# Scores of a pair of heads in one burst, and all value products of a group of blocks in one step

## Chip, cores and metric

One core of one Trainium2 chip runs the kernel in one launch. The metric is the device time of that launch in microseconds, from the runs of the whole kernel; a profiled execution gives the trace. Times without a unit below are microseconds.

## What is computed

An attention with two mixings over the heads (B = 8 batches, H = 12 heads, S = 448 positions, D = 64), and behind it a bilinear expert on the tokens (768 wide, 1024 inside). All inputs and the output are f32.

```python
scores = (1 / sqrt(64)) * q @ k.T                        # per batch and head
scores = einsum('bhij,hg->bgij', scores, w_pre)          # mix the heads
attn   = exp(scores - max); attn = attn / (attn.sum(-1) + 1e-9)
attn   = einsum('bhij,hg->bgij', attn, w_post)           # mix again
x      = attn @ v                                        # 3584 tokens x 768
out    = ((x @ w1) * (x @ w2) @ w3) @ w_out
```

w3 and w_out are multiplied together once ("fold"), so the expert has three products: two "eg" and one "eo".

## The kernel before

**Precision.** TensorE takes a value as f32r (one pass per column) or as plain f32 (two passes). Most f32r products are made in parts: a value is split into a high part (a cast to f32r) and the rest (a subtraction), and a product is the sum of three part products (PAIRS).

**The loop.** The work runs in one loop over n (lines 526 to 589), one iteration per block of IB = 10 query rows of one batch with all 12 heads (120 rows); NB = 45 blocks make a batch, N = 360 all of them. Scores go to DRAM (raw_d, one per batch) and come back one block at a time. In iteration n:
- fetch(n+4) loads the block's scores to r; then the stores and loads that earlier work put on the list "later" are issued, all of them on SyncE's queue.
- softmax(n): VectorE takes a reduce (min) of the mixed scores in PSUM (psm), ScalarE an exponential of them, with the row sum. scale(n-1) prepares the weights w2 of the second mix on VectorE. split_r(n+2) splits r: a VectorE cast (rh) and a GpSimd subtraction (rl). Then the list "soon" (lower parts, casts).
- qk: the scores of a later batch (below). Conversion pieces of the experts' weights stand here too.
- half of the iteration's share of "background" products: the fold at first, then the experts. shares() (line 484) spreads these over the iterations: it sets a weight for each scores and value product in an iteration and fills the rest up to a level.
- post(n-2): four products (eight passes) with e as weights to bank 4; their copy to mt is put on the list "ends".
- av: value products, in some iterations; then the other half of the share, and mix(n+1): three products to psm. Last, the list "ends" copies from PSUM.

The order on every engine is the order in which the program issues (manual_schedule), and each engine works it off in that order. A tile of a pool waits until the one that had its buffer is done with, stores included.

**PSUM** has eight banks, one tag each: 0 and 1 the scores in turn, 2 and 3 psm in turn (n % 2), 4 post (pso), 5 the value products (psa) and a conversion scratch, 6 and 7 the background.

**Scores before** (load_kq, split_kq, qk, lines 141 to 173). load_kq brings [q of head 0 twice, q of head 1 twice, k], 672 KB for a pair. split_kq makes for each head qh and ql, each on both halves of the 128 rows, and kk, with the high part of k in one half and the low part in the other. So a product over 128 rows gives q times (high + low) at once, and a tile of 112 queries takes two products, qh and ql. The 48 tiles of a batch are spread over its iterations, mostly one per iteration. ScalarE copies each to st (two buffers); after two tiles a store goes to "later".

The first batch's scores (qk_first, line 126) are made otherwise: plain f32, head 0 on rows 0 to 63 and head 1 on rows 64 to 127, two banks.

**Values before** (av, line 252): three pairs of heads per step, 2 and 5 iterations after a group of GB = 15 blocks is complete. Head 0 of a pair writes partitions 0 to 63, head 1 64 to 127. Loads of v have three buffers; each used one puts the next load on "later".

Of the kernel before, what the change touches and what calls it, by code (L numbers as in the profile page):

```python
# [4 lines left out]
F32 = mybir.dt.float32  # L5
# [10 lines left out]
HP = H // 2  # L16
# [15 lines left out]
class Kernel:  # L32
    def __init__(self, tc, args, out):
        self.tc, self.nc, self.out = tc, tc.nc, out
        self.kq, self.kq0, self.v, self.wpre, self.wpost = args[:5]
        self.w_src = [w.bitcast(I32) for w in args[5:]]
        self.open = {}
# [88 lines left out]
    def qk_first(self, p, c, banks):  # L126
# [8 lines left out]
        st = (self.qp if p % 2 else self.kp).tile([JT, 2, S], F32, tag="st", name=f"sz{p}_{c}", bufs=2)  # L135
# [5 lines left out]
    def load_kq(self, b, p):  # L141
        t = self.kp.tile([128, 3, S], F32, tag="kq", name=f"kq{b}_{p}")
        self.nc.sync.dma_start(t, self.kq[b, p])
        self.kqs[b, p] = t

    def split_kq(self, b, h, q_lo, k_lo):
        nc, t, s = self.nc, self.kqs[b, h // 2], h % 2
        qh = self.kp.tile([128, S], F32R, tag="qh", name=f"qh{b}_{h}")
        ql = self.kp.tile([128, S], F32R, tag="ql", name=f"ql{b}_{h}")
        kk = self.kp.tile([128, S], F32R, tag="kk", name=f"kk{b}_{h}")  # L150
        a, z = slice(s * D, (s + 1) * D), slice((1 - s) * D, (2 - s) * D)
# [4 lines left out]
        self.parts[b, h] = (qh, ql, kk)  # L156

    def qk(self, b, h, c, i, copy):

        nc = self.nc  # L160
        qh, ql, kk = self.parts[b, h]
        p = self.bank(i, f"psq{b}_{h}_{c}")[:JT, :S]
        cols = slice(c * JT, (c + 1) * JT)
        nc.tensor.matmul(p, qh[:, cols], kk, start=True, stop=False)  # L164
        nc.tensor.matmul(p, ql[:, cols], kk, start=False, stop=True)  # L165
        if c % 2 == 0:
            self.st = self.kp.tile([JT, 2, S], F32, tag="st", name=f"st{b}_{h}_{c}")
        st = self.st
        copy(st[:, c % 2], p)  # L169
        if c % 2 == 0:  # L170
            return None
        rows = self.raw_d[b][(c - 1) * JT:(c + 1) * JT, h, :]
        return lambda: nc.sync.dma_start(rows.rearrange("(c p) j -> p c j", c=2), st)
# [52 lines left out]
    def post(self, n):  # L226
# [8 lines left out]
        copy = nc.scalar.copy if n < LATE else nc.vector.tensor_copy  # L235
# [16 lines left out]
    def av(self, b, a, g):  # L252
        nc, cols = self.nc, self.cols(a)
        W = cols.stop - cols.start
        if g % 3 == 0:
            self.psa = self.bank(5, f"psa{b}_{a}_{g}")[:, :3 * GB * IB].rearrange("p (g i) -> p g i", g=3)
# [6 lines left out]
        if g % 3 == 2:  # L263
# [5 lines left out]
            self.ends.append((5, lambda: nc.scalar.copy(h, q)))  # L269
            self.soon.append((5, lambda: nc.vector.tensor_tensor(l, q, h.bitcast(F32), op=ALU.subtract)))  # L270
        self.later.append(self.load_v)
# [140 lines left out]
    def run(self):  # L412
# [14 lines left out]
        self.vp = self.pool("vp", 3)  # L427
# [7 lines left out]
        for p in range(HP):  # L435
            nc.sync.dma_start(self.kq0s[p], self.kq0[p])
        w, wsc = (self.kp.tile([128, S], F32R, tag="qh", name=x).bitcast(F32)[:GI, :GI] for x in ("wpre_s", "wsc"))
# [23 lines left out]


        loads, splits, qks, avs = {}, {}, {}, {}
        for b in range(1, B):
            first, per, ahead = (12, 26 / 48, 2) if b == 1 else ((b - 1) * NB - 6, 45 / 48, 3)
            for u in range(H * NJ):
# [189 lines left out]
```

## Time and profile before

| | us |
|---|---|
| median of 3 runs (lowest, highest) | 1721.87 (1721.5, 1722.55) |
| the profiled execution's own time | 1720.68 |
| its span in the trace | 1718.9 |
| mean granted clock of TensorE | 0.986 |

In the rows of the profile, PE is TensorE, PEld its weight loads, DVE VectorE, ACT ScalarE, POOL GpSimd, SP (SPq) SyncE, which issues the DMAs. A row names the line, the operation and "written<-read" tiles by their names in the program; "128*112 128x448" is weights of 128 rows and 112 columns under 448 streamed columns. Numbers like 536/627/1087 are the shortest, the median and the longest in ns. TensorE's rows overlap, since a product's row includes the time in which the array drains; the distance of two starts is what a product costs. In a table by stage each engine has its busy time and, in brackets, the number of its instructions.

### The profile page before, as it was taken

To read this page: it belongs to the slowest core of one execution; us is meant where nothing else is said; L and a number is where in the kernel's file an instruction comes from. 1 tells how busy PE (TensorE), PEld (TensorE's weight loads), DVE (VectorE), ACT (ScalarE), POOL (GpSimd) and SP (SyncE) were. 2 spreads that over 40 slices of the span, in tenths; PEclk is the share of its full clock that TensorE was granted. 3 is DMA by queue.
4 is the path that set the end of the run, shared out by engine and by line. 5 is a ranking of instruction groups with operands and counts; after the bars stand their busy time and mean duration, and the time that the engine had idled before them with its cause. 6 is when DMAs were issued, how large, how long until landed. Compare 5 with 4: busy or idle time off the path is not lost.

```text
span 1718.9 us, 30630 instructions
## 1 busy us (share of the span) xinstructions
PE 1648.0 (96%) x10872; PEld 1487.2 (87%) x10872; DVE 935.8 (54%) x2502; ACT 723.6 (42%) x1734; POOL 752.0 (44%) x668
## 2 busy tenths in 40 slices
PE   3889998999999999999999999999999999999999
PEld 1579997788889999899989999899998999998998
DVE  4958667778745555455545555555555555552000
ACT  3867656667643443343433434334433322221010
POOL 1666555667643544444543445345544333231010
PEclk7999999999999999999999999999999999999999
DMA  7979768999888777787778877787768755765764
GB/s 258 294 251 288 244 216 257 289 302 293 265 245 273 241 243 225 240 264 244 247 219 264 253 234 235 246 257 248 244 214 269 226 190 174 236 192 219 263 203 130
DMA packets 186822, 416.51 MB, mean 242 GB/s; under 512 B 17582, under 2 KB 130990, under 8 KB 186670
## 3 DMA queue, kind: packets, MB, share of 16 engines
q1 hardware_dynamic: 186670, 414.57, 76.4%
q8 instruction: 85, 1.39, 0.3%
q14 instruction: 67, 0.55, 0.1%
HBM read 307.54 MB, written 106.95 MB: 241 GB/s over the span
## 4 chain that ended last, share of the span: by engine, by line
PE 72%; DMA 2%; DVE 1%; ACT 0%; issue 0%; POOL 0%; SPq 0%; DVEq 0%; ACTq 0%
PE eg L373 25%; PE eo L398 13%; PE pso L231 13%; PE psa L261 7%; PE psm L199 4%; PE psm L200 3%; PE psm L201 3%; PE psq L164 3%; PE psq L165 3%; DMA wu<-w_d 2%; DVE mn L208 0%; DVE cx L98 0%; DVE ca L95 0%; DVE ca L96 0%; ACT st L169 0%
## 5 line engine op out<-in xcount | busy, mean ns | idle before, releaser
L192 POOL TENSOR_TENSOR rl<-r,rh 120x448 fp32r<-120x448 f32 x360 | 413.2, 1148 | 697.4 <-DVE rh L191 330.5
L211 ACT ACTIVATE e<-psm,mn 120x448 f32<-120x448 f32 x360 | 228.5, 635 | 671.6 <-DVE sa L220 562.5
L373 PE MATMUL eg<-xh,wu 128*128 128x448 f32 x1536 | 478.4, 375 | 4.9 <-ACT wu L103 4.5
L208 DVE TENSOR_REDUCE mn<-psm 120x1 f32<-120x448 f32 x360 | 224.6, 624 | 422.5 <-PE psm L201 422.2
L231 PEld LDWEIGHTS pso<-w,e 120*112 120x112 f32 (+1 forms) x2880 | 348.0, 178 | 47.2 <-ACT mt L237 31.8
L231 PE MATMUL pso<-w,e 120*112 120x120 f32 (+1 forms) x2880 | 360.9, 268 | 15.9 <-ACT mt L237 14.9
L373 PEld LDWEIGHTS eg<-xh,wu 128*128 128x128 f32 x1536 | 284.1, 189 | 28.7 <-ACT wu L103 5.2
L373 PE MATMUL eg<-xl,wu 128*128 128x448 f32 x768 | 284.4, 370 | 0.0
L398 PE MATMUL eo<-eh,wu 128*128 128x448 f32 x768 | 233.9, 375 | 11.0 <-DMA wu<-w_d 11.0
L237 DVE COPY mt<-pso 112x480 f32<-112x480 f32 (+1 forms) x253 | 165.4, 654 | 137.3 <-PE pso L231 136.4
L169 ACT COPY st<-psq 112x448 f32<-112x448 f32 x336 | 173.1, 526 | 16.2 <-DMA raw_d<-st 13.2
L398 PEld LDWEIGHTS eo<-eh,wu 128*128 128x128 f32 x768 | 143.2, 190 | 23.6 <-DMA wu<-w_d 12.9
L261 PE MATMUL psa<-mt,v 112*64 112x150 f32 (+1 forms) x2304 | 156.9, 292 | 1.9 <-DVE xl L270 1.3
L199 PE MATMUL psm<-rh,wph 120*120 120x448 f32 x360 | 139.6, 388 | 18.1 <-DVE rh L191 18.1
L373 PEld LDWEIGHTS eg<-xl,wu 128*128 128x128 f32 x768 | 145.0, 189 | 11.0 <-issue 0.2
L261 PEld LDWEIGHTS psa<-mt,v 112*64 112x64 f32 x2304 | 143.6, 137 | 7.8 <-DVE xl L270 1.6
L191 DVE CAST rh<-r 120x448 fp32r<-120x448 f32 x360 | 146.0, 406 | 0.4 <-DMA r<-raw_d 0.4
L398 PE MATMUL eo<-el,wu 128*128 128x448 f32 x384 | 142.9, 372 | 0.0
L201 PE MATMUL psm<-rl,wph 120*120 120x448 f32 x360 | 132.7, 369 | 0.3 <-POOL rl L192 0.2
L200 PE MATMUL psm<-rh,wpl 120*120 120x448 f32 x360 | 132.5, 368 | 0.0
L386 POOL TENSOR_TENSOR el<-em,eh 128x448 fp32r<-128x448 f32 x64 | 73.8, 1153 | 129.5 <-ACT eh L385 129.5
L164 PE MATMUL psq<-kk,qh 128*112 128x448 f32 x336 | 124.7, 371 | 3.3 <-ACT st L169 3.0
(51 smaller groups left out, 1900.9 us busy)
## 6 DMA issues: line engine op xcount, KB each, us to landing
wu<-w_d SPq DMA_DIRECT2D x112, 768.0 KB, 5.9
r<-raw_d SPq DMA_DIRECT2D x352, 210.0 KB, 3.3
raw_d<-st SPq DMA_DIRECT2D x168, 392.0 KB, 4.1
wu<-w_d SPq DMA_DIRECT2D x96, 512.0 KB, 5.4
v<-v SPq DMA_DIRECT2D x144, 224.0 KB, 4.9
kq<-kq SPq DMA_DIRECT2D x42, 672.0 KB, 7.1
cs<-w SPq DMA_DIRECT2D x32, 384.0 KB, 6.5
w_d<-wu SPq DMA_DIRECT2D x16, 768.0 KB, 5.6
```

The source lines that it names most:

```text
L164: nc.tensor.matmul(p, qh[:, cols], kk, start=True, stop=False)
L169: copy(st[:, c % 2], p)
L192: nc.gpsimd.tensor_tensor(rl[:K], r[:K], rh[:K].bitcast(F32), op=ALU.subtract)
L199: nc.tensor.matmul(p[:K, :S], self.wph[:K, :K], rh[:K], start=True, stop=False)
L200: nc.tensor.matmul(p[:K, :S], self.wpl[:K, :K], rh[:K], start=False, stop=False)
L201: nc.tensor.matmul(p[:K, :S], self.wph[:K, :K], rl[:K], start=False, stop=True)
L208: nc.vector.tensor_reduce(mn[:K], p[:K, :S], axis=AX.X, op=ALU.min)
L211: nc.scalar.activation(e[:K], p[:K, :S], AF.Exp, bias=mn[:K], scale=-1.0, accum_out=sm[:K])
L231: nc.tensor.matmul(p[:, j, :, :w], e[:K, j * JT:(j + 1) * JT], w2[:K, :, :w], start=True, stop=True)
L261: nc.tensor.matmul(self.psa[rows, g % 3, :W], v[:, j, rows], mt[:, j, 2 * g + s, :W], start=(j == 0), stop=(j == NJ - 1))
L373: nc.tensor.matmul(p, w[:, k, x], xs[y][:, k], start=(k == 0 and t == 0), stop=(k == K1 - 1 and t == 2))
L398: nc.tensor.matmul(p, w[:, k % (KF // 2), x], hs[k][y], start=(k == 0 and t == 0), stop=(k == KF - 1 and t == 2))
```

## The change

A pair of heads now has one burst of scores. load_kq brings q and k of the pair once, head 0 on rows 0 to 63 and head 1 on 64 to 127 (448 KB; the same input also serves the first batch). split_kq makes four tiles of 128 rows per pair (two ScalarE casts, two GpSimd subtractions). qk makes all four tiles of 112 queries in a row: for each tile three part products for each head, the two heads on different rows and into different banks, (0, 1) and (3, 5) in turn. ScalarE copies head 0's bank, VectorE head 1's, to st, now with three buffers; the store of tile 0 is issued ahead of tile 3's copies, the others with the next iteration. A burst stands in six iterations per batch, between the first half of the share and post, with a weight of 14 in shares(). There are seven such batches, so 42 bursts.

psm has bank 2 alone. av makes six pairs of heads in one step, 3 iterations after the group is complete, in banks 5 and 3; six buffers for v, whose loads are issued at most two per iteration. In an iteration with a burst ScalarE copies mt.

```diff
     def load_kq(self, b, p):
-        t = self.kp.tile([128, 3, S], F32, tag="kq", name=f"kq{b}_{p}")
+        t = self.kp.tile([128, 2, S], F32, tag="kq", name=f"kq{b}_{p}", bufs=1)
...
-    def split_kq(self, b, h, q_lo, k_lo):
...
-        nc.scalar.copy(qh, t[:, s])
-        nc.scalar.copy(kk[a], t[a, 2])
-        q_lo.tensor_tensor(ql, t[:, s], qh.bitcast(F32), op=ALU.subtract)
-        k_lo.tensor_tensor(kk[z], t[a, 2], kk[a].bitcast(F32), op=ALU.subtract)
...
-        nc.tensor.matmul(p, qh[:, cols], kk, start=True, stop=False)
-        nc.tensor.matmul(p, ql[:, cols], kk, start=False, stop=True)
-        if c % 2 == 0:
-            self.st = self.kp.tile([JT, 2, S], F32, tag="st", name=f"st{b}_{h}_{c}")
...
-        copy(st[:, c % 2], p)
...
+    def split_kq(self, b, p):
+        nc, t = self.nc, self.kqs.pop((b, p))
+        qh, ql, kh, kl = (self.kp.tile([128, S], F32R, tag=x, name=f"{x}{b}_{p}", bufs=1) for x in ("qh", "ql", "kh", "kl"))
+        nc.scalar.copy(qh, t[:, 0])
+        nc.scalar.copy(kh, t[:, 1])
+        nc.gpsimd.tensor_tensor(ql, t[:, 0], qh.bitcast(F32), op=ALU.subtract)
+        nc.gpsimd.tensor_tensor(kl, t[:, 1], kh.bitcast(F32), op=ALU.subtract)
+        self.parts[b, p] = ((qh, kh), (qh, kl), (ql, kh))
+    def qk(self, b, p):
+        nc, parts, stores = self.nc, self.parts.pop((b, p)), []
+        for c in range(NJ):
+            cols = slice(c * JT, (c + 1) * JT)
+            ps = [self.bank(i, f"psq{b}_{p}_{c}_{s}")[:JT, :S] for s, i in enumerate(((0, 1), (3, 5))[c % 2])]
+            for t, (x, y) in enumerate(parts):
+                for s in range(2):
+                    rows = slice(s * D, (s + 1) * D)
+                    nc.tensor.matmul(ps[s], x[rows, cols], y[rows], start=(t == 0), stop=(t == 2))
+            if c == 3:
+                stores.pop(0)()
+            st = self.kp.tile([JT, 2, S], F32, tag="st", name=f"st{b}_{p}_{c}", bufs=3)
+            nc.scalar.copy(st[:, 0], ps[0])
+            nc.vector.tensor_copy(st[:, 1], ps[1])
+            dst = self.raw_d[b][cols, 2 * p:2 * p + 2, :]
+            stores.append(lambda st=st, dst=dst: nc.sync.dma_start(dst, st))
+        self.later += stores
...
-        p = self.bank(2 + n % 2, f"psm{n}")
+        p = self.bank(2, f"psm{n}")
...
-        copy = nc.scalar.copy if n < LATE else nc.vector.tensor_copy
+        copy = nc.scalar.copy if n < LATE or n + 2 in self.qks else nc.vector.tensor_copy
...
+        i = 3 if g > 2 else 5
         if g % 3 == 0:
-            self.psa = self.bank(5, f"psa{b}_{a}_{g}")...
+            self.psa = self.bank(i, f"psa{b}_{a}_{g}")...
...
-        self.later.append(self.load_v)
+        self.v_due += 1
...
-        self.vp = self.pool("vp", 3)
+        self.vp = self.pool("vp", HP)
...
+        avs = {b * NB + (a + 1) * GB + 3: [(b, a, g) for g in range(HP)] for b in range(B) for a in range(NG)}
...
+            first, per = (12, 26 / HP) if b == 1 else ((b - 1) * NB - 6, NB / HP)
+            for p in range(HP):
+                n = first + int(p * per)
+                if n in avs:
+                    n += 1
+                qks[n] = b, p
+                splits[n - 2] = b, p
+                loads[n - 4] = b, p
...
-            other = [len(qks.get(n, [])) * 2 + len(avs.get(n, [])) * 5.4 for n in range(first, last)]
+            other = [(n in qks) * 14 + len(avs.get(n, [])) * 5.4 for n in range(first, last)]
...
+            for _ in range(min(self.v_due, 2)):
+                self.load_v()
+                self.v_due -= 1
...
-            for x in qks.get(n, []):
-                store = self.qk(*x, nq % 2, nc.scalar.copy)
-                nq += 1
-                if store:
-                    self.later.append(store)
...
             advance(share.get(n, 0) // 2)
+            if n in qks:
+                self.qk(*qks[n])
             if 0 <= n - 2 < N:
                 self.post(n - 2)
```

Conversion pieces now skip the iterations of a burst and of a value step, and no longer the one behind a value step.

More of the change, by code (lines that the diff above doesn't have):

```diff
@@ L254, in av @@
         W = cols.stop - cols.start
+        i = 3 if g > 2 else 5
         if g % 3 == 0:
[L256 removed]
+            self.psa = self.bank(i, f"psa{b}_{a}_{g}")[:, :3 * GB * IB].rearrange("p (g i) -> p g i", g=3)
         v, mt = self.vs.pop((b, a, g)), self.mt[b, a]
@@ L511, in run @@
         self.v_list = [(b, a, g) for b in range(B) for a in range(NG) for g in range(HP)]
-        for _ in range(3):
+        self.v_due = 0
+        for _ in range(HP):
             self.load_v()
@@ L547, in run @@
             self.do_later()
-            for x in loads.get(n, []):
-                self.load_kq(*x)
-            for x in splits.get(n, []):
-                self.split_kq(*x, nc.gpsimd, nc.gpsimd)
+            for _ in range(min(self.v_due, 2)):
+                self.load_v()
+                self.v_due -= 1
+            if n in loads:
+                self.load_kq(*loads[n])
+            if n in splits:
+                self.split_kq(*splits[n])
             if n < N:
```

63 lines of the change are left out of this document (16 added, 47 removed).

## The prediction

> **What bounds the kernel now.** I read the profile's page first: busy times (each with its share of the span), then the chain that ended last.
>
> ```profile
> PE 1648.0 (96%) x10872; PEld 1487.2 (87%) x10872; DVE 935.8 (54%) x2502; ACT 723.6 (42%) x1734; POOL 752.0 (44%) x668
> ...
> PE 72%; DMA 2%; DVE 1%; ACT 0%; issue 0%; POOL 0%; SPq 0%; DVEq 0%; ACTq 0%
> PE eg L373 25%; PE eo L398 13%; PE pso L231 13%; PE psa L261 7%; PE psm L199 4%; PE psm L200 3%; PE psm L201 3%; PE psq L164 3%; PE psq L165 3%; DMA wu<-w_d 2%; DVE mn L208 0%; DVE cx L98 0%; DVE ca L95 0%; DVE ca L96 0%; ACT st L169 0%
> ```
>
> The chain is TensorE almost alone, and the products that the change touches are on it: psq (scores) 3% and 3%, psa (values) 7%. The table by stage shows that the long middle has no slack on TensorE:
>
> ```profile
> core 0: us, PE busy (x) PEld busy (x) DVE busy (x) ACT busy (x) POOL busy (x), PEclk, DMA share, GB/s
> ...
> 741.00:1134.00 393.00, 387.91 (x2627) 356.56 (x2626) 209.43 (x577) 153.87 (x375) 177.72 (x155) 1.00 0.78 245
> ```
>
> So a microsecond of TensorE work taken away there comes off the time, and a microsecond in which TensorE waits is added, whatever the other engines' averages are. The question is whether the new order makes TensorE wait. For that I need one iteration of the loop in order of time (start, length, instruction; the number in brackets is idle time before):
>
> ```profile
> 804.44 0.36 PE L201 MATMUL psm<-rl,wph 120*120 120x448 f32 x1
> ...
> 804.64 0.36 PE L164 MATMUL psq<-kk,qh 128*112 128x448 f32 x1
> ...
> 804.84 0.62 DVE L208 TENSOR_REDUCE mn<-psm 120x1 f32<-120x448 f32 x1 [1.31 <-PE psm L201]
> 804.85 0.36 PE L165 MATMUL psq<-kk,ql 128*112 128x448 f32 x1
> ...
> 805.05 0.98 PE L231 MATMUL pso<-w,e 120*112 120x120 f32 x8
> ...
> 805.56 0.63 ACT L211 ACTIVATE e<-psm,mn 120x448 f32<-120x448 f32 x1 [1.87 <-DVE sa L220]
> ...
> 805.96 3.24 PE L261 MATMUL psa<-mt,v 112*64 112x148 f32 x48
> ...
> 806.18 0.52 ACT L169 COPY st<-psq 112x448 f32<-112x448 f32 x1
> 806.26 0.65 DVE L237 COPY mt<-pso 112x480 f32<-112x480 f32 x1
> ...
> 809.13 0.18 PEld L199 LDWEIGHTS psm<-rh,wph 120*120 120x120 f32 x1 [0.20 <-issue]
> 809.13 0.46 PE L199 MATMUL psm<-rh,wph 120*120 120x448 f32 x1
> ```
>
> Starts of 448-column products are 0.20 apart (804.44, 804.64, 804.85, 805.05): I use 0.203 (0.61 / 3). One is shown as 0.36 long because the array drains after it, 0.16. Eight post products take 0.82 (0.98 less the drain), three mix products 0.61. Call the start of L201, the last mix product, X. Then reduce starts at X+0.40, the exponential at X+1.12, and the next copies come at X+1.74 on ScalarE and X+1.82 on VectorE. These two delays decide the change.
>
> **Scores, the work itself.** Before, a pair of heads takes 2 heads x 4 tiles x 2 products = 16 x 0.203 = 3.25. After, 4 tiles x 3 x 2 = 24 products of 64 rows. Do two of them on different rows run together? The first batch's scores have that form:
>
> ```profile
> 61.84 0.36 PE L201 MATMUL psm<-rl,wph 120*120 120x448 f32 x1
> 62.13 0.63 PE L134 MATMUL psz<-kqz 64*112 64x448 f32 x2
> ```
>
> ```profile
> L134 PE MATMUL psz<-kqz x96: 536/627/1087, 4.1 to 91.3; 64*112 64x448 f32 x96
> ```
>
> Two products take 0.63 together, and one has a median of 0.627: they start at the same time. They are plain f32, not the split form of the change, so a pair of the new ones lies between 0.203 (full overlap) and 0.406 (none); I take 0.203, as these rows show overlap without loss. 12 x 0.203 = 2.44.
>
> Going into such tiles costs something: the first psz comes 0.29 after L201 where 0.20 is usual, +0.09, and its own weights are not hidden, 0.627 against 0.536, +0.09. Coming out is shown by the value products: they end their stream near 809.04 (805.96 + 3.24 less the drain), the weights of L199 start at 809.13, +0.09, and L199 is 0.46 long where 0.36 is usual, +0.10. So 0.37 for a burst. Net 2.44 + 0.37 - 3.25 = -0.44; 42 pairs (7 batches x 6): **-18.5**.
>
> For the next steps, VectorE's copy of such a bank and the landing of the first batch's stores, which have the new form of two heads a row, in a stage with more traffic:
>
> ```profile
> L137 DVE COPY sz<-psz x6: 616/622/626, 11.2 to 16.3; 112x448 f32<-112x448 f32 x6
> ...
> DMA to landing us min/median/max: 3.0/4.6/7.9
> ```
>
> **Values.** Their products stay the same; 48 steps of three pairs of heads become 24 of six. A step costs 0.09 + 0.05 in (pso leaves at 805.05 + 0.82 = 805.87, psa starts at 805.96; a 64-column weight load is half of the 0.10) and 0.19 out: 24 x 0.33 = **-7.9**. Six loads of v follow two per block, and the next step is 15 blocks later: hidden; without that cover a step would wait one landing, some 4.6.
>
> **Wait one: banks 0 and 1.** The four tiles share two pairs of banks, and the burst sits straight behind mix. In most batches the share of background products in such a block is nil: the code sets 14 for a burst against a level of (432 + 6 x 14 + 3 x 32.4) / 45 = 13.6. So nothing lies between. Tile 0 streams from X+0.38 to X+0.99, tile 1 to X+1.60. Tile 2 needs tile 0's banks copied, and those copies stand behind the exponential on ScalarE (X+1.74, 0.52) and behind reduce, scale and the cast on VectorE (X+1.82, 0.62): X+2.44. With 0.05 for the signal (L201 ends at 804.80, reduce starts at 804.84) and 0.09 for weights, tile 2 streams at X+2.58: a wait of 0.98. Tile 3's banks come free at X+3.06, before it needs them, and the burst ends at X+3.80. From below the wait is nothing, if the copies kept pace; from above 1.5, where one more ScalarE copy (0.52, a cast of eh) stands in front. I take 0.98: 42 x 0.98 = **+41**.
>
> **Wait two: the store.** Tile 3's copies reuse the buffer of tile 0 (four tiles, three buffers), so both copies wait until tile 0's store has landed.
>
> ```profile
>   ACT st L169: 13.2, 9
> ...
> DMA to landing us min/median/max: 3.1/4.1/7.1
> ```
>
> ScalarE does wait for such stores now (13.2 us, 9 times). The store leaves at X+2.5 and lands 4.1 later, X+6.6. Behind the waiting copy on ScalarE stands the mt copy of that block, which the change puts there:
>
> ```profile
> L237 ACT COPY mt<-pso x107: 481/572/612, 47.3 to 483.5; 112x480 f32<-112x480 f32 x105, 112x384 f32<-112x384 f32 x2
> ```
>
> X+6.6 + 0.52 + 0.57 + gaps = X+7.75; only then is bank 4 free for the next post, X+7.89 with signal and weights. TensorE gets there earlier: X+3.80, out 0.19, post 0.82, mix 0.61, six background products 1.22: X+6.64. It waits 1.25. By the shortest landing, 3.1, the wait is 0.25; by 4.6 it is 1.75. I take 4.1, that of the same stages: 42 x 1.25 = **+52**. On VectorE reduce waits too (to X+7.2), but the next mix comes at X+10. On SyncE the three other stores then block the fetch after next until X+7.3, still two blocks ahead. In 8 pairs before block 50 the share leaves 3 or 4 products (shorter waits), in the 8 between blocks 53 and 107 half a share is only 3 products (longer by 0.6); these I let cancel.
>
> **Hidden edits.** VectorE takes half of the copies (+104, 42 x 4 x 0.62), ScalarE and GpSimd lose some: engines with room (54%, 42% and 44% busy). kq loads shrink by a third; DMA is at 78%, and TensorE waits for it only here:
>
> ```profile
> PE eo L398 <- DMA wu<-w_d: 11.0, 5, 2.6
> ```
>
> Fewer or more such waits: from -16 (all gone, with the clock loss below) to +16; I take 0. The single psm bank needs the exponential (X+1.74) before the next mix, which comes 2.8 or more after X: 0; without that cover, 0.1 a block.
>
> **Sum:** -18.5 - 7.9 + 41 + 52 = +67. Against the profiled execution's 1720.7 this is 1788; the median of the runs shown is 1.2 higher, less than the rounding of the landing.
>
> **The rivals.** (a) *The stores and weights land sooner*, as traffic falls. If a store lands within 2.85 the second wait is gone: 1736; with the weight waits gone as well 1720, not slower. That is the point from which it decides, and the shortest of 168 landings is 3.1. 6%.
>
> (b) *The copies keep pace*, so that wait one is gone: 1747. For it: 0.52 and 0.62 in parallel match a tile's 0.61. Against: in-order queues with the exponential in front. 7%. The Trainium skill, TensorEngine Tiling (Array Packing), section PSUM Bottleneck, says that faster products make the PSUM copy the limit, and to use both ScalarE and VectorE for it. By that remedy the sum would be 1747; the rows say that place in the queue, not copying speed, sets it.
>
> (c) *No overlap of the pairs*, so the change doesn't do what it says: 24 x 0.203 + 0.37 - 3.25 = 1.99 a pair, but then copies are early enough, and TensorE reaches post at X+8.1, after bank 4 is free. +84 - 8: 1796. 5%.
>
> (d) *The clock drops* after a stalled window.
>
> ```profile
> 502.02:505.43 3.41, 1.16 (x6) 0.73 (x4) 1.43 (x5) 2.48 (x6) 1.51 (x2) 1.00 0.89 281
> 505.43:508.84 3.41, 3.13 (x12) 2.98 (x13) 0.38 (x1) 0.13 (x1) 1.87 (x2) 0.50 1.06 291
> ```
>
> ```profile
> 1092.53:1095.94 3.41, 1.75 (x9) 1.24 (x7) 1.43 (x5) 1.91 (x5) 0.99 (x1) 1.00 0.96 296
> 1095.94:1099.35 3.41, 2.60 (x17) 2.48 (x18) 0.66 (x1) 0.69 (x2) 2.41 (x3) 1.00 0.89 273
> ```
>
> A window of 3.41 with TensorE busy 34% was followed by one at half clock, one with 51% was not. Half a window costs 1.7. Waits of 1.0 and 1.25, over 4 apart, leave 60%: no drop; stores that land after 5 would leave less. If all 42 bursts lost one window: 1788 + 71 = 1859. 8%. The Trainium skill, TensorE: Matmul & The Clock Gate, Part 1, wants a whole idle window before the clock falls. By that rule (d) is nothing; the rows show it falls after a window that is a third busy.
>
> My own case has 74%. **Range:** a landing of 3.1 takes 42 off 1788, the weight waits 10 more: 1736. A landing of 4.6 adds 21, and ten windows at half clock 17: 1825. This holds (a) in part, (b) and (c). A measurement tells 0.2% from no change. Faster 3%, the same 3%, slower 94%, from (a) alone and the rest.
>
> **What would show it.** Right: in each burst TensorE waits about 1.0 before the fifth pair for ScalarE or VectorE st; ScalarE waits for DMA raw_d<-st about 42 times, 2 to 3 each; psq pairs 0.2 apart; post waits for ACT mt 42 times. Wrong: few st waits on DMA, a landing under 3, copies of tile 0 ahead of the exponential, or half clock in many slices.

## The result and the profile after

The changed kernel took 1812.48 (median of 6 runs, 1808.32 to 1817.06), the kernel before 1721.68 (6 runs, 1718.83 to 1722.55). The ratio is 1.0533, 95% interval 1.0514 to 1.0552: slower by 5.3%. The profiled execution took 1812.33 (before: 1720.68), so 91.7 have to be found.

First the profile's page after the change, the busy times and the chain that ended last:

```profile
PE 1671.8 (92%) x11208; PEld 1465.1 (81%) x11208; DVE 1020.1 (56%) x2644; ACT 630.0 (35%) x1508; POOL 647.1 (36%) x584
...
PE 60%; DMA 7%; ACT 2%; issue 1%; DVE 1%; POOL 0%; SPq 0%; ACTq 0%
PE eg L374 23%; PE pso L231 11%; PE eo L399 11%; PE psa L262 6%; DMA wu<-w_d 5%; PE psm L199 3%; PE psm L200 3%; PE psm L201 2%; PE psq L165 2%; DMA raw_d<-st 2%; DVE mn L208 1%; ACT st L169 1%; ACT e L211 0%; DMA kq<-kq 0%; ACT mt L237 0%
```

TensorE's share of the chain fell from 72% to 60%. Most of what took its place is DMA (7%, before 2%: the output weights wu<-w_d 5%, the score stores raw_d<-st 2%) and a little ScalarE. Next the clock of TensorE:

```profile
core 0: 1810.5 us, clock 0.976
```

Before it was 0.986. The clock records of these runs hold only whole and half, so 2 x 0.024 x 1810.5 = 87 us of the span are at half clock, against 2 x 0.014 x 1718.9 = 48. If TensorE were busy in all of it, half of the difference, some 19, would be lost.

What TensorE waited for, over the whole span (total, times, longest):

```profile
PE psm L199 <- ACT e L211: 28.1, 31, 3.0
PE psq L165 <- ACT st L169: 21.8, 38, 1.7
...
PE eo L399 <- DMA wu<-w_d: 17.7, 17, 3.5
PE pso L231 <- ACT mt L237: 15.9, 23, 2.0
PE psf L301 <- POOL fw L104: 9.2, 10, 1.5
```

The second row is wait one of the prediction, once in each of 38 of the 42 bursts. The first is a wait that the prediction held to be covered (the mix waits for the exponential), and the last is one that it did not think of (the fold waits for a converted weight). Wait two should show as the fourth row, post for mt. Most of that row is not new; before, it was this:

```profile
PE pso L231 <- ACT mt L237: 14.9, 30, 1.5
```

Between blocks 107 and 305 it grew from nothing to 5.8 in 6 times, where wait two should give 26 x 1.25 = 32.

Where on the span it happened is seen from the three stages between the last mix products of blocks 16 and 50 (fold), 53 and 107 (first experts, the last conversions), 107 and 305 (steady). These are tables by stage of before and of after:

```profile
101.80:260.20 158.40, 156.19 (x1103) 147.28 (x1103) 105.15 (x275) 102.53 (x246) 89.49 (x82) 1.00 0.80 248
270.30:474.80 204.50, 189.58 (x1287) 165.98 (x1288) 158.12 (x413) 141.45 (x336) 135.59 (x122) 0.98 0.91 284
474.80:1337.30 862.50, 851.49 (x5775) 782.64 (x5774) 459.65 (x1261) 337.89 (x822) 388.38 (x338) 0.99 0.78 245
```

```profile
106.40:294.20 187.80, 167.50 (x1216) 148.47 (x1214) 118.64 (x304) 86.87 (x208) 72.25 (x70) 0.98 0.68 201
305.50:542.80 237.30, 208.39 (x1363) 171.31 (x1362) 174.20 (x437) 122.33 (x289) 117.96 (x109) 0.93 0.77 238
542.80:1434.30 891.50, 854.46 (x6026) 762.62 (x6025) 509.85 (x1341) 284.06 (x690) 322.43 (x283) 1.00 0.73 231
```

| blocks | bursts | before | after | difference | by the prediction (67 / 42 a burst) |
|---|---|---|---|---|---|
| 16 to 50 | 7 | 158.4 | 187.8 | +29.4 | +11 |
| 53 to 107 | 8 | 204.5 | 237.3 | +32.8 | +13 |
| 107 to 305 | 26 | 862.5 | 891.5 | +29.0 | +41 |
| the rest | 1 | | | +0.5 | +2 |

So the long steady stage, which the prediction worked through instruction by instruction, cost less than forecast, and the two stages that it let "cancel" cost almost four times as much a burst as the steady one (62.2 / 15 = 4.1 against 29.0 / 26 = 1.1). The stages do not hold quite the same work before and after: by the counts of score and value products in them, the first holds about 5 more after the change, the second and third about 2 more each. In the stage of blocks 53 to 107 TensorE's clock is 0.93 (before 0.98), and TensorE is busy 88% of it.

Now one burst of the steady stage (start, length, instruction, idle time before it):

```profile
845.02 0.37 PE L201 MATMUL psm<-rl,wph 120*120 120x448 f32 x1
...
845.32 0.46 PE L165 MATMUL psq<-kh,qh 64*112 64x448 f32 x2
...
845.62 0.37 PE L165 MATMUL psq<-kl,qh 64*112 64x448 f32 x2
...
845.82 0.36 PE L165 MATMUL psq<-kh,ql 64*112 64x448 f32 x2
...
846.14 0.63 ACT L211 ACTIVATE e<-psm,mn 120x448 f32<-120x448 f32 x1 [3.17 <-DVE sa L220]
...
846.42 0.37 PE L165 MATMUL psq<-kh,ql 64*112 64x448 f32 x2
...
846.77 0.96 ACT L169 COPY st<-psq 112x448 f32<-112x448 f32 x2
...
847.35 0.62 PE L165 MATMUL psq<-kh,qh 64*112 64x448 f32 x2 [0.55 <-ACT st L169]
...
847.53 0.30 SPq L172 DMA_DIRECT2D raw_d<-st  x1
...
848.90 1.07 PE L231 MATMUL pso<-w,e 120*112 120x120 f32 x8
...
850.70 0.53 ACT L169 COPY st<-psq 112x448 f32<-112x448 f32 x1 [1.90 <-PE psm L201]
...
851.13 0.57 ACT L237 COPY mt<-pso 112x480 f32<-112x480 f32 x1
...
851.75 0.89 PEld L231 LDWEIGHTS pso<-w,e 120*112 120x112 f32 x8 [0.31 <-ACT mt L237]
```

Two products of different rows stand in one row (x2), and pairs start 0.20 apart (845.62, 845.82): full overlap. The seventh pair (847.35), the first of the third tile, waits until the first copies, behind the exponential, are done: its first product starts 0.93 behind the sixth pair (846.42) instead of 0.20. The burst takes 3.58 to post, against 12 x 0.203 = 2.44 and 0.2 for going in and out; 0.9 is wait one. The store of tile 0 leaves at 847.53, and tile 3's copy starts at 850.70, 3.2 later. (The releaser named in that row, L201, had long been done; the row's start is where the store's landing lets it go.) ScalarE's mt copy then ends at 851.70, where TensorE, at work on eg until then, is only just ready for post: wait two costs 0.1 here, not 1.25. Over all 42 bursts that store lands 2.9 to 4.8 after its issue, with a median of 3.07, and tile 3's copy starts 0.1 after that. In the four bursts of this stage in which it took 4.1 to 4.8, the post behind it did start 1.1 to 2.0 late: there the chain of wait two ran as predicted (1.25 for a landing of 4.1). The stores as a whole land no sooner than forecast:

```profile
DMA to landing us min/median/max: 2.9/4.6/6.8
```

### The profile page after: what moved, and what is told of

Read it like the earlier page. It is cut to its first block, busy times and chain, and to the rows that moved or that the text cites. A ratio compares the mean times of both kernels' runs of the same rounds, so it can differ in the third digit from the quotient of the medians.

```text
span 1810.5 us, 30929 instructions
## 1 busy us (share of the span) xinstructions
PE 1671.8 (92%) x11208; PEld 1465.1 (81%) x11208; DVE 1020.1 (56%) x2644; ACT 630.0 (35%) x1508; POOL 647.1 (36%) x584
## 4 chain that ended last, share of the span: by engine, by line
PE 60%; DMA 7%; ACT 2%; issue 1%; DVE 1%; POOL 0%; SPq 0%; ACTq 0%
PE eg L374 23%; PE pso L231 11%; PE eo L399 11%; PE psa L262 6%; DMA wu<-w_d 5%; PE psm L199 3%; PE psm L200 3%; PE psm L201 2%; PE psq L165 2%; DMA raw_d<-st 2%; DVE mn L208 1%; ACT st L169 1%; ACT e L211 0%; DMA kq<-kq 0%; ACT mt L237 0%
## 5 line engine op out<-in xcount | busy, mean ns | idle before, releaser
L374 PE MATMUL eg<-xh,wu 128*128 128x448 f32 x1536 | 492.5, 376 | 1.1 <-POOL wu L104 1.1
L231 PE MATMUL pso<-w,e 120*112 120x120 f32 (+1 forms) x2880 | 370.2, 272 | 17.1 <-ACT mt L237 15.9
L399 PE MATMUL eo<-eh,wu 128*128 128x448 f32 x768 | 247.0, 377 | 17.9 <-DMA wu<-w_d 17.7
L237 DVE COPY mt<-pso 112x480 f32<-112x480 f32 x227 | 148.4, 654 | 74.5 <-PE pso L231 73.3
L199 PE MATMUL psm<-rh,wph 120*120 120x448 f32 x360 | 143.7, 399 | 48.5 <-ACT e L211 28.1
L170 DVE COPY st<-psq 112x448 f32<-112x448 f32 x168 | 101.0, 620 | 102.3 <-DMA raw_d<-st 51.0
L191 DVE CAST rh<-r 120x448 fp32r<-120x448 f32 x360 | 157.0, 436 | 0.1
L262 PE MATMUL psa<-mt,v 112*64 112x150 f32 (+1 forms) x2304 | 151.6, 291 | 0.8 <-DVE mt L237 0.7
L201 PE MATMUL psm<-rl,wph 120*120 120x448 f32 x360 | 132.9, 369 | 0.1
L169 ACT COPY st<-psq 112x448 f32<-112x448 f32 x168 | 85.3, 533 | 119.4 <-DMA raw_d<-st 59.1
L223 DVE TENSOR_SCALAR w<-wpo,ri 120x120 f32<-120x120 f32 x360 | 119.6, 332 | 12.6
```

The lines of the kernel that those rows point to most:

```text
L191: nc.vector.tensor_copy(rh[:K], r[:K])
L199: nc.tensor.matmul(p[:K, :S], self.wph[:K, :K], rh[:K], start=True, stop=False)
L201: nc.tensor.matmul(p[:K, :S], self.wph[:K, :K], rl[:K], start=False, stop=True)
L231: nc.tensor.matmul(p[:, j, :, :w], e[:K, j * JT:(j + 1) * JT], w2[:K, :, :w], start=True, stop=True)
L237: self.ends.append((4, lambda: copy(dst, p[:, :, :, :w])))
L262: nc.tensor.matmul(self.psa[rows, g % 3, :W], v[:, j, rows], mt[:, j, 2 * g + s, :W], start=(j == 0), stop=(j == NJ - 1))
```

## The experiments

Theories at the start: A, the two waits of the prediction make up the loss; B, the loss of the two early stages is a wait of its own, from the exponential and the conversions behind which the burst's work is put; C (rival), single terms that were held to be nothing (one psm bank, the later loads of kq) cost it. Line numbers of a kernel with an added line are one higher than those above. The kernel before was run beside each group: 1721.18, 1722.04, 1723.43 and 1721.59.

**A fourth store buffer (e1_buffer).** Tile 3 has a buffer of its own from the fourth batch on (30 bursts), so that nothing waits for the store of tile 0.

```diff
-            st = self.kp.tile([JT, 2, S], F32, tag="st", name=f"st{b}_{p}_{c}", bufs=3)
+            st = self.kp.tile([JT, 2, S], F32, tag="st", name=f"st{b}_{p}_{c}", bufs=3) if c < 3 or b < 3 else \
+                self.k2.tile([JT, 2, S], F32, tag="st", name=f"st{b}_{p}_{c}")
...
+                self.k2 = self.pool("k2", 1, side="right")
```

> The changed kernel with a fourth st buffer for tile 3 in the 30 bursts of batches 3 to 7, so that its copies no longer wait for the store of tile 0. My prediction (wait two costs 1.25 a burst): 30 x 1.25 = 37 us less than the changed kernel's 1812, so about 1775. Rival, from the trace after (the first store of a burst lands after about 3.2 and post waits for ACT mt only 15.9 us in all, 5.8 of them in the steady stage): 4 to 10 us less, about 1805; the ScalarE and VectorE waits for DMA raw_d<-st go all the same.

1804.02; ratio 1.0487 (1.045 to 1.0524). The median is 8 lower than that of the change, and the two intervals overlap; the steady stage is 884.8 instead of 891.5. In the change ScalarE waited for that store in all 42 bursts: 59.1 in 26 times by its list, and 29.9 in 16 times that the list puts to L201. What is left of it here belongs to the 12 early bursts, which still have three buffers:

```profile
ACT st L170 <- DMA raw_d<-st: 27.5, 12, 5.0
```

By the starts in the traces, the posts behind the 26 bursts of the steady stage were 8.4 late in all in the change and 0.1 late here. So wait two exists, but at 26 x 1.25 = 32 for these bursts it was sized about four times too large.

**The burst behind post (e2_behind).** On top of e1, the burst is issued after post, so that post's eight passes lie between the last mix product and the third tile.

```diff
-            if n in qks:
-                self.qk(*qks[n])
             if 0 <= n - 2 < N:
                 self.post(n - 2)
+            if n in qks:
+                self.qk(*qks[n])
```

> The fourth st buffer as before (batches 3 to 7), and the burst issued behind post instead of ahead of it, so that post's 0.82 us lie between mix and the burst and the copies of tile 0 find ScalarE and VectorE free. If wait one is what I say (0.9 a burst, because the copies stand behind the exponential), tile 2 now waits about 0.3: 30 x 0.6 = 18 us less than the same kernel with post behind the burst, perhaps 8 given back in the 12 early bursts with three buffers. Rival (b) turned round: the wait is set by the copying itself or by TensorE's own order, so no change.

1786.1; ratio 1.0373 (1.0352 to 1.0394), 18 below e1. TensorE's waits in the steady stage, first of after, then of this kernel:

```profile
PE eo L399 <- DMA wu<-w_d: 16.6, 15, 3.5
PE psq L165 <- ACT st L169: 14.3, 26, 0.6
PE pso L231 <- ACT mt L237: 5.8, 6, 1.9
```

```profile
PE eo L400 <- DMA wu<-w_d: 19.3, 13, 3.3
PE psm L200 <- ACT e L212: 0.2, 1, 0.2
```

The wait for the copies, 0.55 in each of 26 bursts as TensorE's rows count it, is gone from the list. From its first product to the first one behind it a burst takes 3.02 instead of 3.60 (medians of the steady stage), which for 26 bursts is 15, and the stage is 15.4 shorter than in e1. The place in the queues sets wait one, as the prediction had it; that the copies keep pace (rival b) is out.

**One psm bank in the kernel before (e3_before_psm1).** This is the kernel before, with only that edit of the change.

```diff
-        p = self.bank(2 + n % 2, f"psm{n}")
+        p = self.bank(2, f"psm{n}")
```

> The kernel before with psm in bank 2 alone, nothing else. My prediction took the single bank at 0 us (hidden by the work between). Rival: where an iteration has little background work (blocks 53 to 107), mix waits for the exponential, as the trace after has it (L199 waiting for ACT e: 28.1 us in all, 20.5 in that stage): 15 to 30 us slower than before, about 1740 to 1750, and the same rows appear.

1721.91; ratio 1.0007 (0.9995 to 1.002). By itself it costs nothing. The wait of the mix for the exponential does appear (9.1 in 22 times, none before), while that of post for mt falls from 14.9 to 8.5.

**kq loaded one block earlier (e5_load).** `loads[n - 4]` becomes `loads[n - 5]`.

> The changed kernel with each kq load one iteration earlier (three ahead of its split, not two). My prediction took the loads as hidden: 0 us. Rival: the split stands on ScalarE ahead of the exponential and waits for the load (ACT qh waiting for DMA kq: 43.5 us, 25 times), which delays the exponential, then mix through the one psm bank and post: 5 to 15 us less, with those waits nearly gone.

1808.88; ratio 1.0515 (1.0474 to 1.0556): no difference from the change that can be told. ScalarE's waits for kq, 43.5 in 25 times after the change, are gone, and nothing follows from it. They were a symptom off the path. With these two runs theory C falls for the load, and for the bank in the kernel before; e9 tests the bank in the change.

**The conversion's scratch in SBUF (e4_scratch).** The scratch (ca) lies in bank 5, which tiles 1 and 3 of a burst use too. Here it lies in the tile x in SBUF, worked in place.

```diff
-        a = self.bank(5, f"ca{name}").bitcast(I32)[:, :n]
+        x = self.cs.tile([128, CW], F32, tag="x", name=f"cx{name}")[:, :n]
+        a = x.bitcast(I32)
```

> The changed kernel with the scratch of the weight conversions in SBUF (in the tile of its own result) in place of bank 5, which the burst's odd tiles use. My prediction knew nothing of it: 0 us. Rival: the conversion's three operations on VectorE hold bank 5 while a burst waits (L165 waiting for DVE cx, up to 1.4 each, only before block 107): 5 to 12 us less, about 1802, with the waits for DVE cx gone.

1882.2; ratio 1.0931 (1.0905 to 1.0958): 70 slower than the change, where a gain was expected. The wait for the bank is gone, but the edit brought a larger cost of its own. The same operation, shortest, median and longest in ns, first of after, then of this kernel:

```profile
L95 DVE SCALAR_TENSOR_TENSOR ca<-cs,ca x72: 428/562/564, 17.9 to 510.7; 128x384 int32<-128x384 int32 x64, 128x256 int32<-128x256 int32 x8
```

```profile
L96 DVE SCALAR_TENSOR_TENSOR cx<-cs,cx x72: 424/1390/3451, 17.8 to 578.7; 128x384 int32<-128x384 int32 x64, 128x256 int32<-128x256 int32 x8
```

The last section shows why. This run says nothing on bank 5; what it shows is the price of more work on VectorE in the stages with conversions (+48.6 between blocks 16 and 50, +70.2 between 53 and 107, against before).

**Conversion pieces in every block (e6_pieces).** On top of e4, the pieces no longer skip the blocks of a burst or a value step, so that they are ready sooner for the fold.

```diff
-                if (f < 2 or done >= 2 * KF * 3 * (f - 1)) and n not in avs and n not in qks:
+                if f < 2 or done >= 2 * KF * 3 * (f - 1):
...
-            elif unit_pieces and n not in avs and n not in qks:
+            elif unit_pieces:
```

> The conversion scratch in SBUF, and conversion pieces in every iteration (also those of a burst or of a value step). Theory from the trace after: the fold waits for its weights (L301 waiting for POOL fw and ACT fw, 12.7 us, and the clock falls) because the share between the bursts rose to 16 products an iteration, which leaves exactly the three iterations that three pieces need, and bursts take one away: 12 to 18 us less than with the scratch alone. Rival: the fold is late for another reason (DMA of the words), no change.

1893.84; ratio 1.0997 (1.0958 to 1.1035): slower than e4 by 12 (the intervals touch), and no gain in the fold (+48.7 as in e4). The waits of the fold for converted weights are gone, but TensorE's psq waits for VectorE's copies come in their place (27.1, 13 times). With the slow scratch under it, it can't tell whether the pieces' skipping costs the change anything.

**Value products in steps of three again (e7_av3).** On top of e6.

```diff
-        avs = {b * NB + (a + 1) * GB + 3: [(b, a, g) for g in range(HP)] for b in range(B) for a in range(NG)}
+        avs = {b * NB + (a + 1) * GB + (5 if h else 2): [(b, a, g) for g in range(3 * h, 3 * h + 3)]
+               for b in range(B) for a in range(NG) for h in range(2)}
```

> As the kernel with pieces in every iteration, but with the value products in two steps of three pairs of heads again (2 and 5 iterations behind the group). My prediction: 24 more steps at 0.33 each, 8 us slower than with one step of six. Rival: the step's entry and exit are hidden or the long step costs as much elsewhere: no change.

1902.65; ratio 1.1053 (1.1031 to 1.1074): 8.8 slower than e6. The size is that of the prediction's term (24 x 0.33 = 7.9), but that is a coincidence as far as the traces tell: the two intervals overlap, both kernels carry the slow scratch, and in the long steady stage, which holds more than half of the steps, e6 and e7 take the same (894.8 and 894.2), as other waits moved (post for mt 7.0 in e6 and 20.6 in e7, eo for its weights 14.3 and 3.4). The term can be read from the starts instead. From the last product ahead of a step to the first behind it, a step of 48 value products takes 3.39 in that stage (e7, and the kernel before), a step of 96 takes 6.44 (e6, and the change). One long step saves 2 x 3.39 - 6.44 = 0.34, and 24 of them 8.2.

**Buffer, load, two psm banks together (e8_all).** On top of e6, with the edits of e1 and e5 and the banks of the next experiment.

> The changed kernel with all causes taken away but wait one: scratch in SBUF, pieces in every iteration, kq loads one iteration earlier, the fourth st buffer, and psm in two banks again (the burst takes the psm bank that is idle in its iteration together with 5 for even tiles, 0 and 1 for odd ones; the second half of the values goes to bank 1). If the causes add: 1812 - 20 (psm) - 16 (fold) - 8 (scratch) - 8 (buffer) - 5 (loads) = about 1755, still above before by wait one (42 x 0.9 = 38) less the 26 that the products save. If my prediction's account were right, 1788 - 37 = about 1750 as well, but then the single gains are not seen in the kernels with one edit each.

1871.92; ratio 1.0869 (1.0853 to 1.0885). It is 22 less than e6, but the scratch spoils it as a version.

**Two psm banks in the change (e9_psm2).** The mix has its second bank back; a burst takes (3 - n % 2, 5) and (0, 1), and the second half of the values bank 1.

```diff
-        p = self.bank(2, f"psm{n}")
+        p = self.bank(2 + n % 2, f"psm{n}")
...
-            ps = [... for s, i in enumerate(((0, 1), (3, 5))[c % 2])]
+            ps = [... for s, i in enumerate(((3 - n % 2, 5), (0, 1))[c % 2])]
...
-        i = 3 if g > 2 else 5
+        i = 1 if g > 2 else 5
```

> The changed kernel with psm in two banks again, nothing else but the banks: the burst takes the psm bank that is idle in its iteration together with 5 for even tiles and 0 and 1 for odd ones, the second half of the values goes to bank 1. The single bank cost nothing in the kernel before (ratio 1.0007). Theory: in the changed kernel it does cost, because the iterations without a burst are shorter and the chain mix, reduce, exponential, mix no longer fits when ScalarE has something in front: the 28 us of L199 waiting for ACT e go, about 20 us less than the changed kernel, about 1792. Rival: those waits only show work that is late anyway; then the wait moves to post or eg and the time stays at 1812.

1815.64; ratio 1.0534 (1.0512 to 1.0556): no difference. The mix no longer waits for the exponential (28.1 in the change), but the waits come back at the next places:

```profile
PE pso L231 <- ACT mt L237: 26.8, 39, 2.6
...
PE psq L165 <- DVE cx L98: 12.5, 8, 2.5
```

Post waits for mt, which stands behind the same exponential on ScalarE, and the burst for the scratch in bank 5, which its first tile now needs. Not the bank, but the lateness of the exponential, was what TensorE met.

**No weight for a burst in the share (e10_even).** From the switch to the experts on, a burst counts 0 instead of 14, so that a block with a burst has its background products too, and half of them lie between the mix and the burst.

```diff
-            other = [(n in qks) * 14 + len(avs.get(n, [])) * 5.4 for n in range(first, last)]
+            other = [(n in qks) * (14 if n < SWITCH else 0) + len(avs.get(n, [])) * 5.4 for n in range(first, last)]
```

> The changed kernel with a weight of 0 in place of 14 for a burst in the shares of the background work, from the experts on (34 of 42 bursts). Every iteration then gets the same 6 or 10 products, and half of them lie between mix and the burst. Theory: wait one falls from 0.9 to 0.3 as the copies find the engines free, 34 x 0.6 = 20 us less; and the iterations between blocks 53 and 107 are no longer short, so part of the 21 us that mix waits for the exponential goes as well: 1770 to 1792. By my prediction's account wait two would go too (three or five more products lie ahead of the next post), another 42 less, about 1750. Rival: the burst costs by its own form, not by where it stands: no change.

1791.92; ratio 1.04 (1.0373 to 1.0427), 21 below the change; the steady stage is 877.7, 14 less. TensorE's psq waits for ScalarE's copies fall from 21.8 to 7.3. This is wait one removed in a second way. Its price is seen in the same list: the mix waits for the exponential 39.0 instead of 28.1. Wait two did not go, though the prediction's account said that it would: in the steady stage post waits for mt 6.0 (5.8 in the change). The wait of eo for its weights there falls from 16.6 to 9.5 (11.0 before the change), so its rise in the change goes with the uneven share.

**All of it (e11_even_all).** e10, with the buffer of e1, the loads of e5 and the banks of e9.

> The even shares together with psm in two banks, the fourth st buffer and the earlier kq loads. If the causes add: 1812 - 20 (wait one) - 20 (psm) - 8 (buffer) = about 1764 or less; what is left over the kernel before then stands in the fold stage (blocks 16 to 50), which none of these edits touches and which was 29 us longer. Rival, if one wait only gives way to the next: not under 1780.

1766.37; ratio 1.025 (1.023 to 1.0271): 46 below the change. The steady stage is now 854.5 (from block 107 to 305), 8.0 less than before the change, so the new score and value work is worth something there. But blocks 16 to 50 still take 32.0 more than before and blocks 53 to 107 25.0 more. I read these two stages as bound by VectorE, since the change adds four copies of 0.62 a burst to the conversions. In the change, one block of them without a burst, with a row of the block ahead of it:

```profile
334.77 1.34 DVE L191 CAST rh<-r 120x448 fp32r<-120x448 f32 x1
...
337.21 0.56 DVE L96 SCALAR_TENSOR_TENSOR ca<-cs,ca 128x384 int32<-128x384 int32 x1
...
337.90 0.56 DVE L98 SCALAR_TENSOR_TENSOR cx<-cm,ca 128x384 f32<-128x384 f32 x1
...
338.38 0.61 DVE L381 TENSOR_TENSOR em<-ea,eg 128x448 f32<-128x448 f32 x1
...
338.91 0.62 DVE L208 TENSOR_REDUCE mn<-psm 120x1 f32<-120x448 f32 x1
339.56 0.63 ACT L211 ACTIVATE e<-psm,mn 120x448 f32<-120x448 f32 x1 [3.19 <-DVE mn L208]
...
340.34 0.46 PE L199 MATMUL psm<-rh,wph 120*120 120x448 f32 x1 [2.00 <-ACT e L211]
```

The mix of this block's scores had been ready since about 336, but its reduce stands behind a conversion and the expert's product on VectorE, and so the exponential and the next mix come late: TensorE waits 2.00 in one place. The first row shows a second thing that makes VectorE late: that cast takes 1.34 instead of 0.39 beside a GpSimd subtraction, here of the burst's split (kl, 334.71 to 335.86). It happens in 7 of the 54 blocks of this stage (3 before), some 4 more in all.

**The cast on ScalarE (e12_cast).** e11, with the cast of each row block (rh) on ScalarE up to the steady stage, to test that reading.

```diff
-        nc.vector.tensor_copy(rh[:K], r[:K])
+        (nc.scalar.copy if n < LATE else nc.vector.tensor_copy)(rh[:K], r[:K])
```

> The version with the even share, the buffer, the earlier loads and the two banks, and with the rounding copy of each converted row block (0.39 us of VectorE an iteration) on ScalarE for the blocks before the steady stage. If VectorE is the bound between blocks 16 and 107, the 54 iterations of 53 to 107 give back up to 54 x 0.39 = 21 us and those of 16 to 50 up to 34 x 0.39 = 13 us, less where TensorE is next: 10 to 25 us below the same version without it (1766), so 1742 to 1756. If VectorE's load isn't what lengthens these blocks, or ScalarE's copy stands in front of the exponentials, the time stays at 1766 or rises by up to 10.

1760.62; ratio 1.0232 (1.0218 to 1.0246). It is 5.8 below e11, below the 10 to 25 expected, and the intervals overlap. The two early stages of e11, then of this kernel:

```profile
106.10:296.50 190.40, 170.16 (x1216) 150.28 (x1215) 119.74 (x309) 88.02 (x209) 72.39 (x69) 0.97 0.68 204
303.70:533.20 229.50, 197.81 (x1363) 164.70 (x1362) 178.66 (x445) 124.85 (x295) 119.17 (x110) 0.97 0.82 251
```

```profile
106.80:294.40 187.60, 167.77 (x1215) 150.28 (x1214) 108.19 (x268) 101.23 (x240) 72.17 (x69) 0.97 0.68 204
303.10:529.50 226.40, 196.87 (x1364) 163.95 (x1363) 160.34 (x389) 148.41 (x348) 118.03 (x110) 0.97 0.82 254
```

VectorE had 18.3 less to do between blocks 53 and 107 and 11.6 less between 16 and 50, and these stages became 3.1 and 2.8 shorter. So taking load off VectorE, which is busy 71% of the second one, does not bring the time back. The run does not rule out that ScalarE took over as the bound: the cast made it, which also computes the exponentials, 23.6 and 13.2 busier. I take what is left to be the order inside single blocks. These are this kernel's waits between blocks 53 and 107:

```profile
PE pso L232 <- ACT mt L238: 13.8, 20, 1.8
PE psq L165 <- DVE cx L98: 8.2, 6, 2.2
```

Six of the eight bursts there wait for the conversion's scratch in the bank that they share with it, and post waits for mt as in e9. No version that was tried beats the kernel before; this one is the nearest, 2.3% slower.

## Why the prediction came out as it did

The sign was right and the range held the time (1736 to 1825), near its upper end. The sum was 24 too low, and two errors of opposite sign stand behind it: the steady stage came out 12 cheaper than its share of the sum, the two early stages 38 dearer. That the time still fell into the range owes something to luck, since the range was built on the landing, the weights and the clock, not on the early stages.

- **The scores' work**: right. Pairs overlap in full, 0.20 a pair, so rival (c) is out. Going in and out costs 0.38 a burst where 0.37 was forecast (0.10, 0.10 and 0.09 of start distance, and 0.09 in the post behind).
- **The values' work**: -7.9 forecast, -8.2 by the starts of the steps. The 8.8 between e7 and e6 is not a measure of it.
- **Wait one**: right in place and cause, and near in size: 0.98 a burst forecast, 0.9 read from the burst, in 38 of 42 bursts by the list of waits. The copies start where the prediction put them (846.77 is X+1.75, forecast X+1.74). Two different edits that let the copies come earlier (e2, e10) took most of it away (some 0.3 a burst stays) and brought 18 and 21, though e10 moves other work too. The prediction's sign "before the fifth pair" is a slip: two tiles of three pairs lie ahead of the third tile, so it is the seventh.
- **Wait two**: the step that failed by size. The chain of causes is there (store, tile 3's copies, mt, post), but of +52 only some 8 were real by e1. The term that failed is the landing: the prediction put it at 4.1, the median of the old stores; the new store of tile 0, which leaves ahead of the burst's other three, lands after 3.07 in the median burst. By its own scale (a landing of 3.1 leaves 0.25 a burst) the prediction would have said +10 there. The shortest landing was the right row: the store's circumstances counted, not the median of its kind. Of the signs, ScalarE's 42 waits for the store came (2.1 each), post's 42 waits for mt did not (23, 30 before). The condition of rival (a) came largely true, without its gain: the weights landed sooner too (wu<-w_d 4.8 instead of 5.9, and 4.4 instead of 5.4, in the median), yet eo waited for them longer (16.6 instead of 11.0 in the steady stage, inside the forecast's 16 either way).
- **The early stages**: the step "these I let cancel" failed, and with it "engines with room". Blocks 16 to 107 cost +62 with 15 bursts, where 1.6 a burst gives 24. An engine with 44% of idle time over the span can still be late in the blocks where it has a conversion in front of a reduce. The cover of the single psm bank, "the next mix comes 2.8 or more after X", is gone when the reduce comes late: 28.1 of waits. The prediction priced that loss at 0.1 a block; where it struck, it was 28.1 / 31 = 0.9. But e9 shows that with two banks the same lateness is only met elsewhere. By the starts, the first mix product of a block comes 20 late in all between blocks 53 and 107 (0.4 before), and the score products lose 14 (1 before).
- **The clock**: part of rival (d) came with it. No stalled burst of the steady stage lost the clock (1.00 there), as forecast; between blocks 53 and 107 it fell from 0.98 to 0.93. The first of these two windows of that stage holds the start of the burst of block 76, with waits of 0.61 and 0.85; the second follows it:

```profile
409.27:412.68 3.41, 2.02 (x13) 1.06 (x12) 3.17 (x9) 2.13 (x7) 1.77 (x3) 1.00 0.99 295
412.68:416.09 3.41, 3.34 (x15) 2.77 (x16) 1.40 (x3) 0.98 (x3) 0.98 (x1) 0.50 0.87 258
```

TensorE was busy 59% of the first and the clock still halved, where the prediction took 60% to be safe, from one window with 51% that was not followed by a drop. So the busy share alone does not tell, and the prediction's "no drop" failed in the early bursts. By the clock's rows it took up to 237.3 x 0.07 - 204.5 x 0.02 = 12.5 of TensorE's work there, part of the +32.8.

- **kq and the single psm bank by themselves**: 0 forecast; no difference in e5, e3 and e9.

In the steady stage the measured terms are: scores 26 x (2.44 + 0.38) - 26.4 x 3.25 = -12.5 (the old order had 26.4 pairs there), wait one 26 x 0.9 = 23.4, values -1.4 (14 long steps after, 27 short ones before), wait two 6.7 by e1's stage, and 5.6 more of weight waits: 22 of 29.0. The other 7 stay without an owner.

What stays open: the 29 between blocks 16 and 50. Every version kept 26 or more of it, so neither the store buffer, nor the place of the burst, the banks, the loads or VectorE's cast set it. The largest part is in the fold itself: its 384 products, the same number before and after, follow each other 15 later in all, where the rows show the fold waiting for converted pieces (9.2 for POOL fw and 3.5 for ACT fw, none before). I take it that pieces which skip the burst's block and a share concentrated in the other blocks meet there, but the run that was to test it (e6) had the slow scratch in it, and e10 left the share of these blocks as it was, so this is argued and not shown. In blocks 53 to 107, that a reduce ahead of the conversion would bring the time back was not tried.

## What to carry to other kernels

When work that was spread over all iterations is gathered into bursts, price each stage on its own: the burst block and the blocks that lost the work, with every engine's queue in order of issue. The stage with the most room on average may be the one that pays. Take a transfer's time from one that leaves under the same circumstances, and when a wait is moved by giving it another bank, look at once for the next consumer of the same late result.

## What the runs showed of the hardware

**VectorE beside GpSimd.** In e4 the same operation with both inputs in SBUF took 1.39 (median) instead of 0.56. The timeline of that kernel shows what it stood beside:

```profile
410.18 1.16 POOL L192 TENSOR_TENSOR rl<-r,rh 120x448 fp32r<-120x448 f32 x1 [3.22 <-issue]
410.35 1.40 DVE L96 SCALAR_TENSOR_TENSOR cx<-cs,cx 128x384 int32<-128x384 int32 x1
411.29 1.32 POOL L104 TENSOR_TENSOR wu<-cx,wu 128x384 fp32r<-128x384 f32 x1
411.78 1.25 DVE L97 SCALAR_TENSOR_TENSOR cx<-cs,cx 128x384 int32<-128x384 int32 x1
413.13 0.56 DVE L98 SCALAR_TENSOR_TENSOR cx<-cm,cx 128x384 f32<-128x384 f32 x1
```

410.35 and 411.78 run beside a GpSimd subtraction and take over twice as long; 413.13 has none beside it and takes 0.56. Of the 72 operations of L97, 58 overlap one, with a median of 1.24, and 14 do not, with a median of 0.56; in the change, with one input in PSUM, 70 of 72 of L95 overlap one and the median stays 0.56. The Trainium skill, SBUF — State Buffer, section Who interferes with whom, states this: a VectorE instruction with two SBUF inputs contends with a GpSimd instruction that reads SBUF, one with at most one SBUF input does not, outside the two-port performance modes. These rows agree. The cast at 334.77, with one SBUF input, was lengthened all the same; in which mode it ran is not shown.

**Row pairs.** Products of 64 rows on different halves of the array cost 0.20 a pair at full clock, with a different weight tile in each; the price of going in was 0.10 of start distance (845.02 to 845.32, where 0.20 is usual) and as much again after the first pair (845.32 to 845.62).

**A store ahead of others.** With the same size (392 KB), tile 0's store landed 3.07 after its issue in the median burst, and the three that follow it (issued 1.1, 1.7 and 3.8 later in most bursts) after 4.9; all 168 together have a median of 4.6. What makes the difference was not tested.
